# Token statistics by ACT's running sums, earlier first scores, and a new spread of work in an attention + MLP kernel

## The chip, the cores and the metric

The kernel runs on one core of a Trainium2 chip. The metric is the device time of one execution in microseconds (us). All times here are us unless marked ns. The engines carry the profile's names: PE is TensorE (matmuls), PEld its weight loads, DVE is VectorE, ACT is ScalarE, POOL is GpSimd, SP is SyncE, which here only issues DMAs.

## The reference

The input `x` has 2048 tokens of 512 channels. An attention of 32 heads with 16 channels each looks back over a window of 256 tokens; an MLP of width 1792 runs behind a layer norm; a gate of one number per token mixes the two. All is in fp32.

```python
def _A_ref(x, wqkv, wo):                     # attention
    H = 32; Dh = D // H; W = 256
    qkv = (x @ wqkv).reshape(B, S, 3, H, Dh).transpose(2, 0, 3, 1, 4)
    q, k, v = qkv[0], qkv[1], qkv[2]
    scores = jnp.einsum("bhqd,bhkd->bhqk", q, k) * (Dh ** -0.5)
    mask = (idx[:, None] - idx[None, :] >= 0) & (idx[:, None] - idx[None, :] < W)
    p = softmax(jnp.where(mask[None, None], scores, -1e9))
    o = jnp.einsum("bhqk,bhkd->bhqd", p, v)
    return o.transpose(0, 2, 1, 3).reshape(B, S, D) @ wo

def _B_ref(x, w1, b1, w2, b2):               # MLP
    m = jnp.mean(x, axis=-1, keepdims=True)
    v = jnp.var(x, axis=-1, keepdims=True)
    y = (x - m) / jnp.sqrt(v + 1e-5)
    h = gelu(y @ w1 + b1)                    # tanh form
    return h @ w2 + b2

g = sigmoid((x * gate_w).sum(-1, keepdims=True))
return g * _A_ref(x, wqkv, wo) + (1 - g) * _B_ref(x, w1, b1, w2, b2)
```

## The kernel before, in words

**Numbers.** Each fp32 operand of a matmul is split in a high part (`copy`, L122, on ACT) and the rest (`lo_part`, L119, on DVE or POOL); a product is then three matmuls: high x high, high x low, low x high.

**Three stages.** The *first stage* (0 to about 155 us) makes q, k and v. It is a list of 48 *units*, n = 0 to 47, each of which is one output tile of 12 matmuls (`qk_unit`, L289, or `v_unit`, L319) into one of four PSUM buffers `ps_d`. Between the units other work is put in by a table: `at(n, fn)` lets `fn` run ahead of unit n, and `after(k, fn)` lets it run k units later. The order in which the program calls an engine is the order in which that engine does its work, so these numbers set the order on every engine at once. The *loop* (about 155 to 505) does the attention and the MLP's first product by the letters of `ORDER`: S is a pair of score products for the row maxima, T a pair of transposed scores for the exponentials, P a product with v, f one step of the MLP. One letter is one *spot*. `soon(n, fn)` lets `fn` run n spots later. The *end stage* multiplies by `wo` and `w2`.

**q and k.** `qk_out` (L293) copies and splits a finished tile and stores the parts to DRAM (`put`, L300). `load_stacks` (L325) reads the *stacks* back to the SBUF tile `qk`, in two DMAs at L330; the first call takes the tokens 0 to 511 of the first four heads. `s_pair` (L334) makes the scores of one block of 128 queries with up to 384 keys (L343) in one of two PSUM buffers `ps_x`, and DVE masks (L352) and reduces them (L353) to the maxima `mx`. Ten blocks of the first four heads, two pairs each, are made in the first stage: ahead of the units 16, 19, 22 ... 43.

**The maxima.** After every fourth block `put_max` (L357) splits the maxima on POOL, turns them on DVE (`turn`, `ms`), writes them to DRAM (`put`, L371, `md`) and reads them back as two rows of the stacks (L377, two DMAs, `qk<-md`), from where the T matmuls (L398) take them. In the loop these four steps run at the spots of `CHAIN` after the fourth block: 6, 13, 17 and 34.

**Statistics, gate and y.** `stat_unit(i)` loads 128 tokens (`in_xa`, L440), and three units later DVE makes mean and variance (L444, L445) and the gate's dot product (L446). `stat_end` (L451) has DVE start and POOL finish, in four Newton steps, the inverse root of eight blocks' variances, and stores it. `load_y` (L481) reads mean and inverse root back for 1024 tokens, and then for eight slices (64 channels of each of two halves): load, subtraction of the mean on POOL (L503), multiplication on DVE (L496), copy on ACT, low part on DVE. A slice starts in each unit from 26, and from 34 for the other half of the tokens.

**Other names.** `t2()` (L82) gives the next of `nt` = 15 buffers `t`; whoever takes one waits until its last user is done. `load_w` (L206) loads the other q and k weights (`in_wqk`, L209). `load_w1` loads the MLP's weights, `double` (L308) copies q or k rows within DRAM, `hp` (L635) holds the MLP's first product. SP issues nearly all DMAs, one after the other.

The table's lines that the change touches, and the lines around them:

```python
    at(11, load_consts)
    for c in range(NCH):
        at((12, 22, 33, 44)[c], lambda c=c: load_stacks(0, c * C, C))
    for i in range(NB):
        at(11 + i, lambda i=i: stat_unit(i))
    at(21, lambda: stat_end(0))
    at(29, lambda: stat_end(1))
    at(25, lambda: load_y(0, 0, KT))
    at(33, lambda: load_y(1, 0, KT))
    for qb in range(NB - LAG):
        at(16 + 3 * qb, lambda qb=qb: [s_pair(0, qb, pr) for pr in range(2)])
```

Of the kernel before, what the change touches and what calls it, by code (L numbers as in the profile page):

```python
# [16 lines left out]
AF = mybir.ActivationFunctionType  # L17
ALU = mybir.AluOpType

S = 2048  # L20
D = 512
# [4 lines left out]
KT = D // 64  # L26
FT = F // 128
C = 512
# [6 lines left out]
EPS = 1e-5  # L35
# [13 lines left out]
         "ffTSfffTfSffSPTfSfTffSffTSfffTSfffSSfffTffffTffffTfTPPTTPTfTffTfTffffTfTffPfTTPTfTffTfTfffTffTfPfTTP"  # L49
         "TT")  # L50
LAG = 6
CHAIN = (6, 13, 17, 34)


@with_exitstack
def gated_mix_kernel(ctx, tc: tile.TileContext, xt, x2, wq0, wqk, wv, wo, xa, gw, w1, w2, b1, b2, out):
    nc = tc.nc
    dve, act, pool, pe, sp = nc.vector, nc.scalar, nc.gpsimd, nc.tensor, nc.sync
# [59 lines left out]
    def lo_part(lo, src, hi, eng=dve):  # L118
        eng.tensor_tensor(out=lo, in0=src, in1=f32(hi), op=ALU.subtract)  # L119

    def copy(dst, src):
        act.activation(dst, src, AF.Copy)  # L122
# [4 lines left out]
    def after(k, fn):  # L127
        todo.setdefault(step[0] + k, []).append(fn)
# [17 lines left out]
    stat = dram.tile([2, 2, S // 2], F32, name="stat")  # L146
# [14 lines left out]
    mv = consts.tile([128, NB, 2], F32, name="mv")  # L161
# [3 lines left out]
    get("edge", "edge", 1, (128, 104))  # L165
    open_pool("x", "right")
    open_pool("work")
    nt[0] = 15
    gws = get("work", "gws", 1, (128, D))

    def x8():
        return get("x", "x8", 10, (128, 2048), F32R)
# [152 lines left out]
    def load_stacks(p, a, n):  # L325
        g, j = divmod(p, 2)
        held_cols[p] = a + n
        for t in (1, 0):
            src = view(qkd[g, t], [S, 98], [100 * S, 2], [1, n], off=4 * j * 50 * S + a)
            sp.dma_start(f32(qk[14:112, 2 * t:2 * t + 2, a:a + n]), f32(src))  # L330

    mxs, done = {}, set()
# [105 lines left out]
    def stat_unit(i):  # L438
        s = t2()
        sp.dma_start(s, xa[i])  # L440

        def rest():
            st = small("st", 2, (128, 6))
            dve.bn_stats(st, s)  # L444
            dve.bn_aggr(mv[:, i, :], st)  # L445
            dve.scalar_tensor_tensor(out=s, in0=s, scalar=1.0, in1=gws, op0=ALU.mult, op1=ALU.mult,  # L446
                                     accum_out=z[:, i:i + 1])

        after(3, rest)

    def stat_end(half):  # L451
        ve = small("ve", 2, (128, NB // 2))
        u = small("u", 2, (128, NB // 2))
        m = mv[:, half * 8:half * 8 + 8]
        r = rt[:, half, 1]
        ri = r.bitcast(I32)
        dve.tensor_scalar(ve, m[:, :, 1], EPS, None, op0=ALU.add)
        dve.tensor_scalar(ri, ve.bitcast(I32), 1, None, op0=ALU.logical_shift_right)
        dve.tensor_scalar(ri, ri, -1.0, float(0x5f3759df), op0=ALU.mult, op1=ALU.add)
        for _ in range(4):  # L460
            pool.tensor_tensor(out=u, in0=r, in1=r, op=ALU.mult)
# [3 lines left out]
        pool.tensor_copy(rt[:, half, 0], m[:, :, 0])  # L465
# [12 lines left out]

    ys = {}

    def load_y(cp, s0, s1, gap=2):  # L481
        mr = [t2() for _ in range(2)]
        for j in range(2):
            for e in range(2):
                sp.dma_start(mr[j][64 * e:64 * e + 64], view(stat, [0, 64], [1, C], off=cp * S + j * 2 * C + e * C))

        def one(s):
            if (cp, 0, s // 4) not in ys:
                for k in range(2):
                    ys[cp, k, s // 4] = x8()  # L490
            h, l = (ys[cp, k, s // 4][:, s % 4 * C:s % 4 * C + C] for k in range(2))
            x = t2()
            sp.dma_start(x, x2[cp, :, s * C:(s + 1) * C])

            def rest():
                dve.tensor_tensor(out=x, in0=x, in1=mr[1], op=ALU.mult)  # L496
                copy(h, x)

            def fin():
                lo_part(l, x, h)  # L500
                done.add(("y", cp, s))

            after(2, lambda: pool.tensor_tensor(out=x, in0=x, in1=mr[0], op=ALU.subtract))  # L503
            after(3, rest)
            after(4, fin)

        for s in range(s0, s1):
            after(1 + (s - s0) * gap // 2, lambda s=s: one(s))

    w1t = {}  # L510

    def load_w1(f, eng=pool):
        w, raw = [wt(), wt()], t2()
        w1t[f] = w
        sp.dma_start(raw, w1[f])
# [28 lines left out]
    rest = [QK(g, t, c) for c in range(NCH) for g in range(1, NG) for t in range(2)]  # L544
# [4 lines left out]
    def at(n, fn):  # L549
        plan.setdefault(n, []).append(fn)  # L550
# [5 lines left out]
    for i in range(4):  # L556
        at((3, 5, 6, 8)[i], lambda i=i: pool.memset(vs[:, 4 * i:4 * i + 4], 1.0))
    at(2, masks)
    at(11, load_consts)
    for g in range(NG):  # L560
        at((8, 16, 20, 24)[g], lambda g=g: gaps(g))
    for c in range(NCH):
        at((12, 22, 33, 44)[c], lambda c=c: load_stacks(0, c * C, C))
    for i in range(NB):
        at(11 + i, lambda i=i: stat_unit(i))
    at(21, lambda: stat_end(0))
    at(29, lambda: stat_end(1))
# [278 lines left out]
    for n in range(len(seq)):  # L846
        tick()
        for k in (n + 6,):
            c, f = item(k)
# [4 lines left out]
        c, f = item(n + 1)  # L854
# [59 lines left out]
```

## Time and profile before

| | |
|---|---|
| median of 3 runs | 712.82 (710.83 to 714.23) |
| the profiled execution | 716.88, of which its span 715.2 |
| granted TensorE clock, mean | 0.992 |
| PE busy | 694.1 (97%), 5740 matmuls |
| DVE busy | 484.3 (68%) |
| ACT busy | 365.8 (51%) |
| POOL busy | 270.6 (38%) |
| DMA | 137.92 MB, mean 193 GB/s |

How the rows of the profile read: in the lists of groups and of waits a row has the engine, the source line, the operation and `out<-in` by the program's names (with buffer numbers left out), then how many there were, their busy time and the mean ns of one, and behind the last bar the idle time ahead of them and what ended it. In a timeline a row begins with the start and the length in us, and a bracket holds the idle time just before it and its releaser. SPq is SP's queue of DMA issues. In a row of windows, each engine has its busy time and its count of instructions; behind them stand the granted TensorE clock, the DMA engines' share, and GB/s.

### The profile page before, as it was taken

The page shows a single profiled execution, that of the slowest core. Times are in us where ns is not written, and L with a number is a line of the kernel's source. Part 1 is how long each engine was busy: PE and PEld are TensorE (multiplying, and loading weights), DVE is VectorE, ACT ScalarE, POOL GpSimd, SP SyncE. Part 2 cuts the span into 40 slices and gives each one's busy share as a digit, 9 for nine tenths or more (in the row PEclk, how much of TensorE's full clock was granted, in tenths as well). Part 3 has the DMA queues.
Part 4 walks back from the last instruction along what each step waited for, and adds up shares of the span by engine and source line. Part 5 has one row for each costly group of instructions (what it writes and reads, how often), then busy time and mean ns, then how long its engine had stood idle before and what let it go on. Part 6 is the DMA issues. An engine that isn't in the chain of part 4 may idle for free.

```text
span 715.2 us, 15880 instructions
## 1 busy us (share of the span) xinstructions
PE 694.1 (97%) x5740; PEld 542.3 (76%) x5740; DVE 484.3 (68%) x996; ACT 365.8 (51%) x581; POOL 270.6 (38%) x631
## 2 busy tenths in 40 slices
PE   9999989799999989999999999999999999999997
PEld 6877767577677767777777778777677788888886
DVE  7639877877786858868767677784375745735554
ACT  6422223247668667667775767768543413224121
POOL 9600173506467456556654656658200000000000
PEclk9999999999999999999999999999999999999999
DMA  8998959677556657656867564544775544442531
GB/s 316 337 287 247 297 179 270 194 220 221 192 179 194 189 196 217 190 189 175 238 186 204 158 202 149 173 120 151 239 241 152 175 140 144 153 138 99 191 112 59
DMA packets 102533, 137.92 MB, mean 193 GB/s; under 512 B 13912, under 2 KB 53528, under 8 KB 102328
## 3 DMA queue, kind: packets, MB, share of 16 engines
q1 hardware_dynamic: 97848, 128.79, 57.7%
q10 hardware_dynamic: 4608, 8.13, 3.8%
q8 instruction: 46, 0.75, 0.4%
q14 instruction: 31, 0.25, 0.1%
HBM read 81.53 MB, written 54.30 MB: 190 GB/s over the span
## 4 chain that ended last, share of the span: by engine, by line
PE 65%; DMA 15%; DVE 7%; SPq 5%; issue 3%; ACT 2%; POOL 2%; ACTq 0%; DVEq 0%; POOLq 0%
PE ps_b L622 20%; PE ps_a L833 16%; PE ps_b L417 11%; PE ps_b L398 7%; PE ps_b L343 6%; PE ps_o L812 6%; DMA t<-in_wqk 2%; DMA qk<-t 2%; DMA qk<-md 1%; DMA v<-in_xt 1%; DVE t L496 1%; DMA t<-stat 1%; DMA t<-hp 1%; DVE t L119 1%; SPq L300 1%
## 5 line engine op out<-in xcount | busy, mean ns | idle before, releaser
L622 PE MATMUL ps_b<-x,w 64*128 64x512 f32 x1344 | 215.6, 398 | 0.5 <-ACT p L400 0.2
L402 POOL TENSOR_SCALAR_AFFINE_SELECT p<-p 128x256 f32<-128x256 f32 x344 | 132.4, 414 | 111.2 <-ACT p L400 109.8
L400 ACT ACTIVATE p<-ps_b 128x768 f32<-128x768 f32 (+2 forms) x184 | 137.6, 770 | 45.8 <-PE ps_b L398 37.7
L833 PE MATMUL ps_a<-x,t 128*128 128x512 f32 x648 | 151.0, 390 | 0.3 <-DVE t L682 0.2
L353 DVE TENSOR_REDUCE mx<-ps_b 128x2 f32<-128x512 f32 x208 | 144.1, 693 | 7.2
L833 PEld LDWEIGHTS ps_a<-x,t 128*128 128x128 f32 x648 | 121.2, 188 | 27.3 <-DVE t L119 1.2
L622 PEld LDWEIGHTS ps_b<-x,w 64*128 64x128 f32 x1344 | 132.3, 188 | 12.0 <-issue 2.8
L352 DVE COPY_PREDICATED ps_b<-tri,ps_b 128x256 f32<-128x256 uint8 x208 | 88.3, 425 | 55.3 <-PE ps_b L343 39.5
L398 PE MATMUL ps_b<-qk 64*128 64x384 f32 (+5 forms) x512 | 92.1, 347 | 5.8 <-DMA qk<-md 4.9
L289 PE MATMUL ps_d<-x,w 128*128 128x512 f32 x360 | 88.5, 398 | 0.0
L343 PE MATMUL ps_b<-qk 62*128 62x384 f32 (+3 forms) x472 | 86.4, 347 | 0.6 <-ACT v L122 0.5
L289 PEld LDWEIGHTS ps_d<-x,w 128*128 128x128 f32 x360 | 67.9, 191 | 16.0 <-issue 1.7
L417 PE MATMUL ps_b<-p,v 128*32 128x256 f32 (+1 forms) x1376 | 74.4, 329 | 0.9 <-ACT p L400 0.9
L398 PEld LDWEIGHTS ps_b<-qk 64*128 64x128 f32 (+1 forms) x512 | 52.1, 186 | 26.3 <-issue 9.5
L122 ACT ACTIVATE t<-ps_b 128x512 f32<-128x512 f32 (+1 forms) x112 | 52.0, 491 | 39.1 <-PE ps_b L417 33.8
L402 POOL TENSOR_SCALAR_AFFINE_SELECT x<-x 128x256 f32<-128x256 f32 x136 | 52.1, 410 | 38.1 <-ACT x L400 37.5
L400 ACT ACTIVATE x<-ps_b 128x768 f32<-128x768 f32 (+2 forms) x72 | 55.3, 778 | 19.4 <-PE ps_b L398 15.2
L417 PEld LDWEIGHTS ps_b<-p,v 128*32 128x32 f32 x1376 | 38.7, 109 | 26.7 <-ACT p L400 4.1
L343 PEld LDWEIGHTS ps_b<-qk 62*128 62x128 f32 (+1 forms) x472 | 47.6, 187 | 14.9 <-issue 3.6
L119 DVE TENSOR_TENSOR t<-t,t 128x512 fp32r<-128x512 f32 x70 | 48.5, 692 | 14.6 <-ACT t L122 11.6
L122 ACT ACTIVATE t<-t 128x512 fp32r<-128x512 f32 x16 | 10.1, 632 | 79.1 <-DVE t L800 54.8
L678 ACT ACTIVATE t<-t,b1s 128x512 f32<-128x512 f32 x56 | 38.0, 715 | 24.0 <-DMA t<-hp 23.5
(81 smaller groups left out, 662.3 us busy)
## 6 DMA issues: line engine op xcount, KB each, us to landing
qk<-qk SPq DMA_DIRECT2D x112, 196.0 KB
t<-hp SPq DMA_DIRECT2D x56, 256.0 KB
hp<-t SPq DMA_DIRECT2D x52, 256.0 KB
qk<-t SPq DMA_DIRECT2D x48, 256.0 KB
osc<-t SPq DMA_DIRECT2D x31, 256.0 KB
t<-in_w SPq DMA_DIRECT2D x28, 256.0 KB
w<-w SPq DMA_DIRECT2D x28, 256.0 KB
qk<-t ACTq DMA_DIRECT2D x24, 256.0 KB
```

What stands on the lines that cost most here:

```text
L119: eng.tensor_tensor(out=lo, in0=src, in1=f32(hi), op=ALU.subtract)
L122: act.activation(dst, src, AF.Copy)
L289: pe.matmul(o, a[:, dt * 128:(dt + 1) * 128], b[:, dt * C:(dt + 1) * C], start=n == 0, stop=n == 11)
L343: pe.matmul(o[:, e, :n], qs[pr][r:k, qb * 128:qb * 128 + 128], ks[pr][r:k, t0:t0 + n], start=True, stop=True)
L352: dve.copy_predicated(o[:, :, :128], tri, o[:, :, 256:384])
L353: dve.tensor_reduce(m, o[:, :, :256], mybir.AxisListType.X, ALU.max)
L398: pe.matmul(o[:, e, :w], ks[pr][r:k, kb * 128:kb * 128 + 128], qs[pr][r:k, kb * 128:kb * 128 + w], start=True, stop=True)
L400: act.activation(pt[:, :, :w], o[:, :, :w], AF.Exp, scale=0.25)
L402: pool.affine_select(out=pt[:, :, a:a + 128], in_=pt[:, :, a:a + 128], pattern=[[0, 2], [sgn, 128]], base=b, channel_multiplier=-sgn, comp ...
L417: pe.matmul(a[32 * h:32 * h + 32, at:at + w], vs[:, kb, v:v + 32], pts[p, kb][:, h, fr:fr + w], start=n == 0, stop=n == len(parts) - 1, sk ...
L622: pe.matmul(o[:, e], w[kt // 4][r:r + 64, k, m:m + 128], y[r:r + 64, a:a + C], start=n == 0, stop=n == 23)
L833: pe.matmul(accs[c][b], x[:, b * 128:(b + 1) * 128], w, start=f == 0 and n == 0, stop=f == FT - 1 and n == 2)
```

## The change

The mean and variance of a token are made on ACT by two activations with running sums: a copy scaled by -1/512, whose sum is the negative mean, and a square with that as bias, whose sum is 512 times the variance. Their full outputs go to a new tile `waste`, for which the ring of `t` buffers has 14 instead of 15. The dot product stays on DVE, one unit later. `stat_end` scales the variance on DVE, and POOL does three Newton steps in place of four; the subtraction of the mean becomes an addition. The blocks of tokens are loaded one unit earlier, from unit 10. The two tables of statistics for y are read at units 25 and 32, and the y slices start at the units 24, 25, 26, 28, 29, 30, 31, 32 and 33 to 40, with lags of 3 and 2 units up to the subtraction. The stacks are loaded ahead of the units 11, 19, 28, 44 instead of 12, 22, 33, 44, and the ten blocks of scores are made ahead of the units 14, 16, 18, 21, 23, 25, 28, 30, 33, 36. The MLP's first two weights are loaded one unit earlier. In the loop the maxima are read back 28 instead of 34 spots after their block.

```diff
-CHAIN = (6, 13, 17, 34)
+CHAIN = (6, 13, 17, 28)
...
-    nt[0] = 15
+    nt[0] = 14
     gws = get("work", "gws", 1, (128, D))
+    waste = get("work", "waste", 1, (128, D))
...
         sp.dma_start(s, xa[i])
 
-        def rest():
-            st = small("st", 2, (128, 6))
-            dve.bn_stats(st, s)
-            dve.bn_aggr(mv[:, i, :], st)
+        def sums():
+            act.activation(waste, s, AF.Copy, scale=-1.0 / D, accum_out=mv[:, i, 0:1])
+            act.activation(waste, s, AF.Square, bias=mv[:, i, 0:1], accum_out=mv[:, i, 1:2])
+
+        def dot():
             dve.scalar_tensor_tensor(out=s, in0=s, scalar=1.0, in1=gws, op0=ALU.mult, op1=ALU.mult,
                                      accum_out=z[:, i:i + 1])
 
-        after(3, rest)
+        after(3, sums)
+        after(4, dot)
...
-        dve.tensor_scalar(ve, m[:, :, 1], EPS, None, op0=ALU.add)
+        dve.tensor_scalar(ve, m[:, :, 1], 1.0 / D, EPS, op0=ALU.mult, op1=ALU.add)
...
-        for _ in range(4):
+        for _ in range(3):
...
-    def load_y(cp, s0, s1, gap=2):
-        mr = [t2() for _ in range(2)]
+    mr = {}
+
+    def load_mr(cp):
+        mr[cp] = [t2() for _ in range(2)]
         for j in range(2):
             for e in range(2):
-                sp.dma_start(mr[j][64 * e:64 * e + 64], view(stat, [0, 64], [1, C], off=cp * S + j * 2 * C + e * C))
+                sp.dma_start(mr[cp][j][64 * e:64 * e + 64], view(stat, [0, 64], [1, C], off=cp * S + j * 2 * C + e * C))
...
-            after(2, lambda: pool.tensor_tensor(out=x, in0=x, in1=mr[0], op=ALU.subtract))
-            after(3, rest)
-            after(4, fin)
-
-        for s in range(s0, s1):
-            after(1 + (s - s0) * gap // 2, lambda s=s: one(s))
+        after(lag, lambda: pool.tensor_tensor(out=x, in0=x, in1=mr[cp][0], op=ALU.add))
+        after(lag + 1, scale)
+        after(lag + 2, low)
...
-    at(11, load_consts)
+    at(10, load_consts)
...
-        at((12, 22, 33, 44)[c], lambda c=c: load_stacks(0, c * C, C))
+        at((11, 19, 28, 44)[c], lambda c=c: load_stacks(0, c * C, C))
     for i in range(NB):
-        at(11 + i, lambda i=i: stat_unit(i))
+        at(10 + i, lambda i=i: stat_unit(i))
     at(21, lambda: stat_end(0))
     at(29, lambda: stat_end(1))
+    at(25, lambda: load_mr(0))
+    at(32, lambda: load_mr(1))
+    for i in range(KT):
+        at((24, 25, 26, 28, 29, 30, 31, 32)[i], lambda i=i: load_y(0, i, 3))
+        at(33 + i, lambda i=i: load_y(1, i, 2))
...
-    at(25, lambda: load_y(0, 0, KT))
-    at(33, lambda: load_y(1, 0, KT))
-    at(39, lambda: load_w1(0, dve))
-    at(42, lambda: load_w1(1, dve))
+    at(38, lambda: load_w1(0, dve))
+    at(41, lambda: load_w1(1, dve))
     for qb in range(NB - LAG):
-        at(16 + 3 * qb, lambda qb=qb: [s_pair(0, qb, pr) for pr in range(2)])
+        at((14, 16, 18, 21, 23, 25, 28, 30, 33, 36)[qb], lambda qb=qb: [s_pair(0, qb, pr) for pr in range(2)])
```

Three places show how rows move. Line numbers of the changed kernel are one to five higher than those of before for the same operation. The first place is SP's queue behind its first 28 rows, which are the same in both: `in_wqk` are weights of q and k, `in_xa` blocks of tokens, `qk_1_66` and `qk_0_67` stored q and k parts, `qk_79` the SBUF tile of the stacks. Before:

```order
L435 DMA gws_99<-in_gw 128x512
L436 DMA b1s<-in_b 128x14
L440 DMA t_463<-in_xa 128x512
L209 DMA t_466<-in_wqk 128x512
L330 DMA qk_79<-qk_1_66 98x2x512
L330 DMA qk_79<-qk_0_65 98x2x512
L440 DMA t_486<-in_xa 128x512
```

The same place after:

```order
L436 DMA gws_99<-in_gw 128x512
L437 DMA b1s<-in_b 128x14
L441 DMA t_448<-in_xa 128x512
L331 DMA qk_79<-qk_1_66 98x2x512
L331 DMA qk_79<-qk_0_65 98x2x512
L441 DMA t_468<-in_xa 128x512
L210 DMA t_471<-in_wqk 128x512
```

The stacks stand one row higher: one `in_wqk` that was ahead of them is now behind them, with a block of tokens between.

The second place is DVE from the last short instruction of the second half's `stat_end` (on `rt`). `x_161` and the like are high and low parts of y, `t_869` and `t_891` the inverse roots read back, `ps_d` the units' outputs, `ps_x` score pairs. Before:

```order
L459 TENSOR_SCALAR rt<-rt 128x8
L119 TENSOR_TENSOR x_162_912<-t_913,x_161_911 128x512
L496 TENSOR_TENSOR t_938<-t_938,t_869 128x512
L119 TENSOR_TENSOR t_1067<-ps_d_1053,t_1066 128x512
L119 TENSOR_TENSOR x_162_912<-t_938,x_161_911 128x512
L496 TENSOR_TENSOR t_962<-t_962,t_869 128x512
L467 STREAM_TRANSPOSE ms_1028<-rt 128x32
L352 COPY_PREDICATED ps_x_1080<-tri,ps_x_1080 128x2x128
L353 TENSOR_REDUCE mx_588<-ps_x_1080 128x2
```

After:

```order
L462 TENSOR_SCALAR rt<-rt 128x8
L119 TENSOR_TENSOR x_144_863<-t_896,x_143_862 128x512
L501 TENSOR_TENSOR t_930<-t_930,t_891 128x512
L353 COPY_PREDICATED ps_x_1057<-tri,ps_x_1057 128x2x128
L354 TENSOR_REDUCE mx_543<-ps_x_1057 128x2
L353 COPY_PREDICATED ps_x_1062<-tri,ps_x_1062 128x2x128
L354 TENSOR_REDUCE mx_543<-ps_x_1062 128x2
L119 TENSOR_TENSOR t_1086<-ps_d_1072,t_1085 128x512
L119 TENSOR_TENSOR x_144_863<-t_930,x_143_862 128x512
L470 STREAM_TRANSPOSE ms_1031<-rt 128x32
L369 STREAM_TRANSPOSE ms_1068<-nm_1067 128x32
```

Before, two multiplications of y (L496) stand between the end of the statistics and the next score pair; after, one (L501) does, and the next multiplication comes behind the transposes.

The third place is SP around the tenth write of maxima in the loop. `md` are the maxima in DRAM, `osc` and `hp` stored results, `w<-w` a swap of the MLP's weights within SBUF, the row at L310 or L311 a `double`. Before:

```order
L371 DMA md_2934<-ms_2933 4x32x32
L430 DMA osc<-t_2883 128x512
L519 DMA w_2854<-w_2853 64x1024 x2
L635 DMA hp<-t_3052 128x512
L635 DMA hp<-t_3054 128x512
L330 DMA qk_79<-qk_1_68 98x2x256
L330 DMA qk_79<-qk_0_67 98x2x256
L310 DMA qk_1_70<-qk_1_70 16x8x512
L377 DMA qk_79<-md_2934 2x2x512 x2
```

After:

```order
L372 DMA md_2911<-ms_2910 4x32x32
L431 DMA osc<-t_2862 128x512
L378 DMA qk_79<-md_2911 2x2x512 x2
L521 DMA w_2833<-w_2832 64x1024 x2
L640 DMA hp<-t_3031 128x512
L640 DMA hp<-t_3033 128x512
L331 DMA qk_79<-qk_1_68 98x2x256
L331 DMA qk_79<-qk_0_67 98x2x256
L311 DMA qk_1_70<-qk_1_70 16x8x512
```

The reading back of the maxima stands seven DMAs higher, one other row behind the write.

More of the change, by code (lines that the diff above doesn't have):

```diff
@@ L479, in gated_mix_kernel, with load_y, scale, low @@
     ys = {}
-    def load_y(cp, s0, s1, gap=2):
-        mr = [t2() for _ in range(2)]
+    mr = {}
+    def load_mr(cp):
+        mr[cp] = [t2() for _ in range(2)]
         for j in range(2):
             for e in range(2):
-                sp.dma_start(mr[j][64 * e:64 * e + 64], view(stat, [0, 64], [1, C], off=cp * S + j * 2 * C + e * C))
[L487 to L503, printed above, removed]
-            after(3, rest)
-            after(4, fin)
-        for s in range(s0, s1):
-            after(1 + (s - s0) * gap // 2, lambda s=s: one(s))
+                sp.dma_start(mr[cp][j][64 * e:64 * e + 64], view(stat, [0, 64], [1, C], off=cp * S + j * 2 * C + e * C))
+    def load_y(cp, s, lag):
+        if (cp, 0, s // 4) not in ys:
+            for k in range(2):
+                ys[cp, k, s // 4] = x8()
+        h, l = (ys[cp, k, s // 4][:, s % 4 * C:s % 4 * C + C] for k in range(2))
+        x = t2()
+        sp.dma_start(x, x2[cp, :, s * C:(s + 1) * C])
+        def scale():
+            dve.tensor_tensor(out=x, in0=x, in1=mr[cp][1], op=ALU.mult)
+            copy(h, x)
+        def low():
+            lo_part(l, x, h)
+            done.add(("y", cp, s))
+        after(lag, lambda: pool.tensor_tensor(out=x, in0=x, in1=mr[cp][0], op=ALU.add))
+        after(lag + 1, scale)
+        after(lag + 2, low)
     w1t = {}
```

## Prediction

> All times are us, and a "unit" is the stretch of 12 matmuls between two positions of the first stage. I read the page's first part, then TensorE's waits, then windows with the granted clock, then the timeline at each wait.
>
> **What bounds the kernel now.**
>
> ```profile
> PE 694.1 (97%) x5740; PEld 542.3 (76%) x5740; DVE 484.3 (68%) x996; ACT 365.8 (51%) x581; POOL 270.6 (38%) x631
> ```
>
> TensorE is idle for 715.2 - 694.1 = 21.1. The change removes no matmul, so it can win only PE's waits and slow matmuls behind them, and it can lose by making waits. Who ends them (total, times, longest):
>
> ```profile
> PE ps_x L343 <- DVE mx L353: 6.3, 7, 2.1
> PE ps_b L398 <- DMA qk<-md: 4.9, 3, 2.5
> PE ps_b L398 <- DVE ms L368: 0.6, 1, 0.6
> PE ps_x L343 <- DMA qk<-qk: 0.5, 1, 0.5
> ```
>
> The first group is the first stage's score pairs, which have two PSUM buffers and wait until DVE has reduced the pair before. The next two are the returns of the maxima (the 0.6 I count with them: a return of maxima was in flight there). The last is the first load of the stacks. Windows (length, then busy time of PE, PEld, DVE, ACT, POOL, granted clock, DMA share, GB/s):
>
> ```profile
> 45.00:51.00 6.00, 5.49 (x25) 4.21 (x24) 2.75 (x6) 1.72 (x3) 0.00 (x0) 1.00 1.04 248
> 51.00:94.00 43.00, 42.98 (x195) 34.00 (x196) 36.46 (x102) 9.47 (x16) 6.36 (x21) 1.00 0.92 285
> 94.00:143.00 49.00, 42.58 (x180) 32.41 (x179) 37.75 (x58) 14.27 (x28) 26.52 (x34) 0.97 0.69 204
> 139.50:144.00 4.50, 4.50 (x15) 3.52 (x14) 3.67 (x5) 1.24 (x3) 1.78 (x1) 0.62 0.56 166
> 389.00:393.00 4.00, 4.00 (x24) 3.72 (x24) 2.43 (x6) 2.15 (x5) 1.88 (x6) 0.57 0.64 205
> ```
>
> Until 94 PE is full; 94 to 143 holds the DVE waits; and three times the clock falls to half for some 3.4 (the first and the last are the two last rows: a mean of 0.62 over 4.5). PE's own rows show what such a dip costs and what stands ahead of it:
>
> ```profile
> 44.88 2.88 PE L319 MATMUL ps_d<-wv,x 128*128 128x512 f32 x12
> 47.60 2.88 PE L289 MATMUL ps_d<-x,w 128*128 128x512 f32 x12
> 51.02 0.44 PE L343 MATMUL ps_x<-qk 62*128 62x128 f32 x4 [0.54 <-DMA qk<-qk]
> ...
> 138.08 0.44 PE L343 MATMUL ps_x<-qk 62*128 62x384 f32 x2 [2.15 <-DVE mx L353]
> ...
> 139.52 4.61 PE L289 MATMUL ps_d<-x,w 128*128 128x512 f32 x12
> ...
> 253.02 0.69 PE L398 MATMUL ps_b<-qk 64*128 64x384 f32 x2 [2.55 <-DMA qk<-md]
> ...
> 387.18 0.45 PE L398 MATMUL ps_b<-qk 64*128 64x384 f32 x2 [1.44 <-DMA qk<-md]
> ```
>
> A unit is 47.60 - 44.88 = 2.72. Twelve matmuls took 4.61 at half clock against 2.88: 1.7 lost, each of three times behind a wait of 1.44 or more (the three rows with brackets from 138 on).
>
> Why DVE is late, from its rows and POOL's:
>
> ```profile
> 102.75 1.75 DVE L496 TENSOR_TENSOR t<-t,t 128x512 f32<-128x512 f32 x1 [3.46 <-POOL t L503]
> 104.55 0.39 DVE L352 COPY_PREDICATED ps_x<-tri,ps_x 128x256 f32<-128x256 uint8 x1
> ```
>
> ```profile
> 95.69 0.57 POOL L461 TENSOR_TENSOR u<-rt 128x8 f32<-128x8 f32 x1 [1.13 <-DVE rt L459]
> ...
> 101.28 0.19 POOL L465 COPY rt<-mv 128x8 f32<-128x8 f32 x1
> 101.43 5.42 POOL L503 TENSOR_TENSOR t<-t,t 128x512 f32<-128x512 f32 x4
> ```
>
> DVE stood 3.46 before a y slice, whose subtraction stood on POOL behind the Newton steps (95.69 to 101.47), and the score pair behind that slice is reduced only from 104.55. With 37.75 busy of the 49 from 94 to 143, and idle times of its own between, DVE doesn't get that back: the longest of PE's waits for it stands at 138.
>
> **The change, part by part.** Durations (busy, mean ns):
>
> ```profile
> L444 DVE BATCH_NORM_STATS2 st<-t 128x6 f32<-128x512 f32 x16 | 10.9, 683 | 6.0 <-DMA t<-in_xa 6.0
> L445 DVE BATCH_NORM_AGGREGATE mv<-st 128x2 f32<-128x6 f32 x16 | 2.9, 182 | 0.6
> L446 DVE SCALAR_TENSOR_TENSOR t<-t,gws 128x512 f32<-128x512 f32 x16 | 10.8, 678 | 0.0
> L446 DVE DVE_READ_ACCUMULATOR t<-t,gws 128x1 f32 x16 | 1.3, 82 | 0.0
> L496 DVE TENSOR_TENSOR t<-t,t 128x512 f32<-128x512 f32 x16 | 17.5, 1094 | 3.5 <-POOL t L503 3.5
> L119 DVE TENSOR_TENSOR x<-t,x 128x512 fp32r<-128x512 f32 x16 | 11.8, 739 | 3.4 <-ACT x L122 3.4
> L119 DVE TENSOR_TENSOR t<-ps_d,t 128x512 fp32r<-128x512 f32 x22 | 15.1, 685 | 6.0 <-ACT t L122 6.0
> L353 DVE TENSOR_REDUCE mx<-ps_x 128x2 f32<-128x512 f32 x16 | 11.1, 693 | 0.5
> L122 ACT ACTIVATE x<-t 128x512 fp32r<-128x512 f32 x16 | 10.1, 632 | 42.1 <-DVE t L496 42.1
> L678 ACT ACTIVATE t<-t,b1s 128x512 f32<-128x512 f32 x56 | 38.0, 715 | 24.0 <-DMA t<-hp 23.5
> ```
>
> *Sums on ACT.* DVE loses 16 x (0.68 + 0.18) = 13.8. ACT gains 32 instructions: a copy like the 0.63 row, and a square with a bias per partition like the 0.715 row. No row of ACT has a running sum; its price lies between nothing and DVE's read of an accumulator, 0.08. The nearest row is the latter, so 16 x (0.63 + 0.72 + 0.16) = 24. They fall into units 13 to 28, where ACT was busy for 9.5 of 43, and a `qk` copy behind them may be late by three units, since there are four `ps_d` buffers: nothing on the path. If an `xa` load lands late, ACT stands where DVE stood (6.0 above); the same three units cover it.
>
> Here the Trainium skill speaks against the change: ScalarE: Activation LUTs, Rules for kernel authors, sends adding and multiplying to VectorE. By it the move trades 13.8 of DVE for 24 of ACT, some 10 lost. The windows above decide otherwise: from 94 on DVE ends PE's waits and ACT has room.
>
> *Fewer Newton steps* take 4 of 16 operations from POOL, about (101.28 - 95.69) / 4 = 1.4 each half. *The y slices* now leave a gap behind the second half's Newton steps: the slice after them is multiplied two units later, so the 3.46 goes.
>
> *DVE's account from unit 28*, starting 1.3 behind PE (copy 0.6, low part 0.69), with dot 0.76, multiply 1.09, low part of y 0.74, two reductions 2.2 (0.69 and the 0.39 of 104.55, twice), and 0.9 for the short ones (an estimate: six, none above L445's 0.18): the pair of unit 28 is reduced at 5.3, of 30 at 13.2, of 33 at 20.8. PE (2.72 a unit, 0.6 a pair) asks for them at 6.0, 14.8 and 23.6. So no wait. If each multiply took 1.75, as beside POOL above, it would be 6.0, 15.2, 24.1: up to 0.8 in all. I keep 0.5: **-6.3 + 0.5 = -5.8**, and the dip behind the 2.15 goes: **-1.7**. After unit 36 DVE is some two units behind, four `ps_d` buffers cover it.
>
> *First pairs at unit 14, stacks at unit 11.* SyncE before:
>
> ```profile
> 40.03 0.43 SPq L440 DMA_DIRECT2D t<-in_xa  x1
> 40.51 0.45 SPq L209 DMA_DIRECT2D t<-in_wqk  x1
> 41.06 0.83 SPq L330 DMA_DIRECT2D qk<-qk  x2
> ```
>
> Its first 28 rows are the same in both programs and stand one behind the other, so moving the stacks one unit up moves them past one DMA only, the `in_wqk` of 256 KB. At the 285 GB/s of 51 to 94 that is 0.9, at the 248 of 45 to 51 1.06; I take 0.9. They landed at 51.02, so now at 50.1. PE however asks for them at the start of unit 14, 44.88: a wait of 5.2 in place of 0.5, **+4.7**. The bounds: 0 were the queue empty, 5.6 were nothing won. A dip follows, as it did behind shorter waits: **+1.7**. Behind it nothing is hurt: DVE, ACT and the DMAs gain on PE.
>
> On dips the Trainium skill (TensorE: Matmul & The Clock Gate, The HAM clock gate) asks for an idle window of about 3.4, free-running. Here waits of 1.44 to 2.55 were enough, so the measurement decides; it bears on rival (5).
>
> *The other stack loads* (units 19, 28) keep four and five units to their pairs; the maxima of the first two blocks are sent earlier, and SP stands there when idle. *One `t` buffer less*: the tightest new user is the `y` load of unit 35, which waits for the subtraction of that unit and is used two units later: nothing, at worst one unit of SP. *w1 a unit earlier*: nothing.
>
> *Maxima read back at 28.* 30 of 32 returns move six spots up on SP, some 1.7 (350 for the 1202 letters):
>
> ```profile
> 239.81 0.58 SPq L371 DMA_DIRECT2D md<-ms  x1
> 242.11 0.36 SPq L430 DMA_DIRECT2D osc<-t  x1
> ...
> 249.40 1.37 SPq L377 DMA_DIRECT2D qk<-md  x2
> ...
> 379.42 0.60 SPq L371 DMA_DIRECT2D md<-ms  x1
> ...
> 384.35 1.35 SPq L377 DMA_DIRECT2D qk<-md  x2
> ```
>
> At 249.40 the return came behind seven transfers that now stand behind it; it can go at about 243, and the 2.55 ends, as do the 0.6 and the remaining 4.9 - 2.55 - 1.44 = 0.9, which have the same order. The 1.44 stays: there SP waited until 384.35 for the write itself, which no order helps. **-4.1**, and the dip behind the 2.55: **-1.7**.
>
> **Sum.** The profiled execution took 716.88: -5.8 - 1.7 + 4.7 + 1.7 - 4.1 - 1.7 = -6.9, 710.0. The median of the runs is 712.82, 4.1 below it. The first four terms (-1.1) hang on queue order and should recur; the last two (-5.8) hang on when a DMA landed, and the lower median says that a usual run has less of them. I take half: 712.82 - 1.1 - 2.9 = **708.8**.
>
> **Rivals.** (1) SyncE becomes the bound: a return directly behind its write stands until that lands, up to 4.9 above, and the stack loads behind it are late. It decides the time once a load has less than that left between its issue and its use. Against it: of all first uses of stacks only the very first waits now (the 0.5 of the waits' list), though the list doesn't say by how much the others make it. Three loads late by 2, each with a dip: 711.7 + 3 x 3.7 = 722.8, where 711.7 = 712.82 - 1.1. (2) The first stacks are hidden anyway: 708.8 - 6.4 = 702.4; the full DMA share at 45 to 51 (1.04) speaks against it. (3) The change leaves DVE behind all the same, since its account is within 1 of PE at unit 30: without the 7.5 of the first two terms, 716.3. (4) The returns win nothing, as other transfers hold them: 711.7. (5) No dip follows the wait at unit 14, as none followed most of the waits listed above (three dips in all): 708.8 - 1.7 = 707.1. By the clock gate's rule that depends on where a free-running window falls, and a wait of 5.2 holds a whole one of 3.4 in about half of the cases.
>
> **Chances.** Likeliest 0.40, (1) 0.13, (2) 0.08, (3) 0.14, (4) 0.16, (5) 0.09. The range leaves out (1) alone: 702 to 717. The likeliest case alone is 706 to 711. About 0.5%, 3.6, is what a measurement tells from no change: faster means below 709.26. That holds (2), (5) and six tenths of the likeliest: 0.41; slower, above 716.4, (1) and half of (3): 0.20; the rest 0.39.
>
> **What would show it.** Right: one PE wait of about 5 at some 45, ended by `qk<-qk`, with half clock behind; no L343 wait on DVE over 0.5; `md` waits below 2 in all. Wrong: L343 waits on DVE of several us remain; stack waits appear after 160; or PE runs through unit 14, which would break the largest loss in the sum.

## The result, and the profile after

The changed kernel takes 719.21 us (median of 8 runs, 716.28 to 721.91), the kernel before 713.07 in the same runs (8, 710.83 to 715.74). The ratio is 1.0082, with a 95% interval of 1.0055 to 1.0109: 5.9 us slower. The forecast was 708.8, with a range of 702 to 717, so the time lies outside of the range and on the other side of no change.

The profiled execution took 721.91 (span 720.2). Its first part, and TensorE's waits (total, times, longest):

```profile
PE 698.6 (97%) x5740; PEld 541.7 (75%) x5740; DVE 472.7 (66%) x964; ACT 388.5 (54%) x645; POOL 268.6 (37%) x623
```

```profile
PE ps_x L344 <- DMA qk<-qk: 4.2, 1, 4.2
PE ps_b L344 <- ACT p L401: 3.1, 1, 3.1
...
PE ps_b L399 <- DMA qk<-md: 1.4, 2, 1.2
PE ps_d L290 <- ACT v L122: 1.3, 2, 0.9
PE ps_d L320 <- DVE t L119: 1.1, 1, 1.1
...
PE ps_x L344 <- DVE mx L354: 0.6, 1, 0.6
...
PE ps_d L290 <- DVE t L119: 0.3, 1, 0.3
```

Most of what the prediction named as signs of being right is there: one wait at unit 14 for the stacks (4.2), 1.4 in place of 4.9 for the return of the maxima, and 0.6 in place of 6.3 for DVE's maxima in the first stage, a little above the 0.5 that it had set. What it did not name are the rows that are new: 2.7 for `ps_d`, the units' output buffers, and 3.1 for ACT's exponentials. PE's rows show where they stand:

```profile
49.81 0.59 PE L344 MATMUL ps_x<-qk 62*128 62x128 f32 x4 [4.16 <-DMA qk<-qk]
...
137.45 5.78 PE L290 MATMUL ps_d<-x,w 128*128 128x512 f32 x24 [0.36 <-ACT v L122]
...
144.34 3.06 PE L320 MATMUL ps_d<-wv,x 128*128 128x512 f32 x12 [1.12 <-DVE t L119]
148.31 3.03 PE L290 MATMUL ps_d<-x,w 128*128 128x512 f32 x12 [0.91 <-ACT v L122]
151.62 3.04 PE L290 MATMUL ps_d<-x,w 128*128 128x512 f32 x12 [0.29 <-DVE t L119]
...
166.53 0.69 PE L344 MATMUL ps_b<-qk 62*128 62x384 f32 x2 [3.12 <-ACT p L401]
```

Two waits have a stretch of half clock behind them (windows; the third last number is the granted clock):

```profile
49.50:54.00 4.50, 4.19 (x14) 3.38 (x15) 1.30 (x8) 2.06 (x5) 0.00 (x0) 0.62 1.04 386
...
166.00:171.00 5.00, 4.47 (x24) 3.88 (x26) 2.36 (x5) 2.21 (x4) 2.62 (x8) 0.50 0.51 177
```

The first of these stretches lasted 3.4, as each of the three before the change did. The second lasted 6.8 (from 166 to 174 the granted clock was 0.57), so it costs about 3.4 and not 1.7.

Since PE does the same 5740 matmuls in both, one can ask at which time each is begun. That tells where the 5.0 between the two spans came from:

| PE begins | before | after | after is behind by |
|---|---|---|---|
| unit 13 | 42.16 | 42.69 | 0.5 |
| unit 17 | 54.23 | 60.74 | 6.5 |
| unit 29 | 89.89 | 97.72 | 7.8 |
| unit 44 | 143.97 | 144.34 | 0.4 |
| unit 47, the last | 152.16 | 154.70 | 2.5 |
| matmul 700, early in the loop | 163.81 | 171.71 | 7.9 |
| matmul 3392 in the loop | 392.63 | 395.53 | 2.9 |
| end of the span | 715.2 | 720.2 | 5.0 |

Three of the steps were forecast. The first is 6.0 lost at unit 14 (6.4 in the sum): 3.6 more of wait (4.16 in place of 0.54), 1.7 of half clock, and some 0.6 for the matmuls of one more block of scores. The second is 7.4 won back by unit 44, of which 1.3 are the matmuls of two blocks of scores that the changed kernel makes ahead of unit 29 already, so 6.1 of waits and dips (7.5). The third is 5.0 won in the loop, where the returns of the maxima are (5.8, of which the forecast took half). Three steps were not forecast: 2.1 behind unit 44, 5.4 at the start of the loop, and a drift that has no wait to its name, with 0.5 ahead of unit 13, some 0.6 of the 1.3 between the units 17 and 29 (the rest is the other block of scores), and 2.1 behind matmul 3392.

### The profile page after: what moved, and what is told of

Same layout as the page of the kernel before. It is cut to its first block, busy times and chain, and to the rows that moved or that the text cites. A ratio compares the mean times of both kernels' runs of the same rounds, so it can differ in the third digit from the quotient of the medians.

```text
span 720.2 us, 15939 instructions
## 1 busy us (share of the span) xinstructions
PE 698.6 (97%) x5740; PEld 541.7 (75%) x5740; DVE 472.7 (66%) x964; ACT 388.5 (54%) x645; POOL 268.6 (37%) x623
## 3 DMA queue, kind: packets, MB, share of 16 engines
q10 hardware_dynamic: 4608, 8.13, 3.7%
## 4 chain that ended last, share of the span: by engine, by line
PE 67%; DMA 12%; DVE 8%; SPq 5%; ACT 4%; issue 3%; POOL 1%; ACTq 1%; DVEq 0%; POOLq 0%
PE ps_b L627 19%; PE ps_a L838 16%; PE ps_b L418 11%; PE ps_b L399 6%; PE ps_b L344 6%; PE ps_o L817 6%; DMA qk<-qk 3%; DVE t L501 2%; DVE x L119 2%; ACT t L122 1%; PE ps_d L290 1%; SPq L301 1%; DMA md<-ms 1%; ACT x L122 1%; DMA qk<-t 1%
## 5 line engine op out<-in xcount | busy, mean ns | idle before, releaser
L627 PEld LDWEIGHTS ps_b<-x,w 64*128 64x128 f32 x1344 | 132.5, 188 | 12.3 <-issue 2.8
L290 PE MATMUL ps_d<-x,w 128*128 128x512 f32 x360 | 86.9, 396 | 1.6 <-ACT v L122 1.3
L344 PEld LDWEIGHTS ps_b<-qk 62*128 62x128 f32 x472 | 47.6, 187 | 19.8 <-ACT p L401 5.9
L119 DVE TENSOR_TENSOR t<-t,t 128x512 fp32r<-128x512 f32 x70 | 48.5, 693 | 14.9 <-ACT t L122 11.6
```

What stands on the lines that cost most here:

```text
L290: pe.matmul(o, a[:, dt * 128:(dt + 1) * 128], b[:, dt * C:(dt + 1) * C], start=n == 0, stop=n == 11)
L344: pe.matmul(o[:, e, :n], qs[pr][r:k, qb * 128:qb * 128 + 128], ks[pr][r:k, t0:t0 + n], start=True, stop=True)
L627: pe.matmul(o[:, e], w[kt // 4][r:r + 64, k, m:m + 128], y[r:r + 64, a:a + C], start=n == 0, stop=n == 23)
```

## The experiments

Each ratio is to the kernel before, from runs on the same chip; its interval is of 95%. The median of the kernel before lay between 713.1 and 715.9 from one set of runs to the next, so kernels are compared by their ratios.

**The first scores.** Theory Y was that the chain of y on DVE and ACT bounds the second half of the first stage, so that time lost at unit 14 is lost for good; rival Q that SyncE's queue does, and hides it.

```diff
-        at((14, 16, 18, 21, 23, 25, 28, 30, 33, 36)[qb], ...
+        at((16, 17, 18, 21, 23, 25, 28, 30, 33, 36)[qb], ...
```

> The changed kernel, with the first two blocks of scores ahead of units 16 and 17 instead of 14 and 16; all else as in the changed kernel. Theory Y: the second half of the first stage is bound by y's chain (multiply on DVE, copy on ACT, the unit's own copy behind it on ACT, low parts on DVE: 3.6 us a slice in the changed kernel against 2.72 a unit), so what is lost at unit 14 moves the chain's first slice and with it the end of the stage one to one. It expects the 4.2 wait and the dip behind it to go, the first multiplication at about 91.5 instead of 97.6, the stage's end some 6 earlier, and 713 us. Rival Q: the end of the stage is set by SyncE, whose loads of y stand behind stores of q and k that wait for DVE; then PE's lost time at unit 14 is hidden by the later waits, the stage ends within 1.5 of now, and the time is 717.5 to 719.5.

Measured: 713.21, ratio 1.0000 (0.9975 to 1.0024), 0.8% under the changed kernel. The time lost at the first scores is not hidden, and Q as it was put is refuted. But the way there isn't quite the one expected, as PE's rows of this run show:

```profile
50.99 0.44 PE L344 MATMUL ps_x<-qk 62*128 62x128 f32 x4
51.36 3.03 PE L290 MATMUL ps_d<-x,w 128*128 128x512 f32 x12
56.09 0.83 PE L344 MATMUL ps_x<-qk 62*128 62x256 f32 x4 [1.70 <-DVE mx L350]
56.84 4.61 PE L320 MATMUL ps_d<-wv,x 128*128 128x512 f32 x12
```

The stacks are in time for unit 16, but three blocks of scores in three units make PE wait 1.70 for DVE, with a unit at half clock (4.61) behind it. PE began unit 17 at 56.84 against 60.74, and unit 47 at 150.45 against 154.70, so 3.9 gained became 4.3; the waits for `ps_d` remained (0.8, 0.7 and 0.3). The wait for the exponentials was gone, which this edit does not explain by itself; that is taken up at the last run.

**Score and stack tables alone**, on the kernel before:

```diff
-        at((12, 22, 33, 44)[c], lambda c=c: load_stacks(0, c * C, C))
+        at((11, 19, 28, 44)[c], lambda c=c: load_stacks(0, c * C, C))
...
-        at(16 + 3 * qb, lambda qb=qb: [s_pair(0, qb, pr) for pr in range(2)])
+        at((14, 16, 18, 21, 23, 25, 28, 30, 33, 36)[qb], lambda qb=qb: ...
```

> The kernel before, with the changed tables of score blocks and stack loads alone. Theory Y: PE waits 4 to 5 us at unit 14 with a dip behind it, y's chain starts 6 later, and the whole comes out at 718 to 720, as the changed kernel does: the other parts of the change are then worth about nothing together. Rival: the waits of the score pairs for DVE (6.3) are slack that takes the loss up, since DVE gets more time: 712 to 715.

Measured: 720.68, ratio 1.0088 (1.0060 to 1.0117). PE's waits:

```profile
PE ps_b L398 <- DMA qk<-md: 7.3, 5, 2.2
PE ps_x L343 <- DMA qk<-qk: 4.6, 1, 4.6
...
PE ps_x L343 <- DVE mx L353: 2.0, 2, 1.4
...
PE ps_d L319 <- DVE t L119: 1.1, 1, 1.1
```

The two tables alone cost what the whole change costs. And they alone turn 4.3 of the 6.3 of waiting for the maxima away, while waits for `ps_d` come up: earlier scores let PE run ahead of DVE until the four output buffers are full, and there it stands instead. (The waits for the returned maxima, 7.3 in this execution against 4.9, are longer as well.)

**The maxima's return**, undone in the changed kernel and done alone in the kernel before:

```diff
-CHAIN = (6, 13, 17, 28)
+CHAIN = (6, 13, 17, 34)
```

> The changed kernel with the maxima read back at spot 34 as before. If the earlier reading back was worth the 4 us that the prediction gave it at most, 722 to 724 and md waits of 3 to 5 us; if it was worth half, 721; if it is worth nothing or costs (its wait for its own write holds up SyncE), 717 to 719.5.

Measured: 724.67, ratio 1.0116 (1.0059 to 1.0172), with 4.9 of waits for the returned maxima (`qk<-md`) in three places. The interval overlaps that of the changed kernel (1.0055 to 1.0109), so this run alone doesn't tell the two apart.

> The kernel before with the maxima read back at spot 28; nothing else. The run with spot 34 in the changed kernel makes the earlier reading back worth about 5 there. If that carries over: md waits under 2 in the loop, 708 to 710. If it is worth something only behind the other changes, 713 to 715. If SyncE standing at its own write costs stack loads, over 716.

Measured: 711.05, ratio 0.9940 (0.9912 to 0.9969): a gain of 4.3, between 2.2 and 6.3. The md waits of this run are in one row:

```profile
PE ps_b L398 <- DMA qk<-md: 0.4, 1, 0.4
```

The earlier return has a price, too. All nine kernels here that read the maxima back at spot 28 make PE wait for stacks in the loop (`ps_b` <- `qk<-qk`), 0.5 to 3.0 in all and 1.8 in this one; the lists of the six with spot 34 show no such wait.

**ACT's running sums alone**, on the kernel before (with the tile `waste`, 14 `t` buffers, and the dot product, the loads and the constants moved as in the change):

```diff
-        after(3, rest)
+        after(3, sums)
+        after(4, dot)
```

> The kernel before with mean and variance by ACT's running sums alone (and what hangs on it: the tile of waste, 14 t buffers, the dot product a unit later, the token loads and constants a unit earlier, the sign of the mean); four Newton steps, old tables. The prediction's account of DVE would take some 8 of its 13.8 us off ahead of unit 28 and the waits of the score pairs with them: 706 to 709. Theory Y (what counts is the ping-pong of DVE and ACT per slice of y from unit 29 on, and POOL's Newton steps, none of which this touches): the waits for the maxima stay above 4 us, 712 to 716.

Measured: 717.24, ratio 1.0033 (1.0008 to 1.0058), above both ranges. The waits for the maxima did fall, from 6.3 to 2.4, as the prediction's account had it and theory Y had not; PE began unit 47 2.3 earlier than before. But the time is not shorter: the returns took 6.2 in this execution, and matmuls were slower, as the runs on the place in SBUF show below.

**The copy of y.** In the changed kernel's rows DVE and ACT take turns. DVE:

```profile
140.63 1.79 DVE L501 TENSOR_TENSOR t<-t,t 128x512 f32<-128x512 f32 x1
143.60 0.69 DVE L119 TENSOR_TENSOR t<-ps_d,t 128x512 fp32r<-128x512 f32 x1 [1.18 <-ACT t L122]
144.20 0.68 DVE L119 TENSOR_TENSOR x<-t,x 128x512 fp32r<-128x512 f32 x1
144.80 1.78 DVE L501 TENSOR_TENSOR t<-t,t 128x512 f32<-128x512 f32 x1
```

ACT:

```profile
142.45 0.63 ACT L122 ACTIVATE x<-t 128x512 fp32r<-128x512 f32 x1 [3.06 <-DVE t L501]
142.99 0.58 ACT L122 ACTIVATE t<-ps_d 128x512 fp32r<-128x512 f32 x1
```

ACT copies a y slice only when DVE has multiplied it, the unit's own output waits behind that copy on ACT, and DVE waits for the unit's output: 144.80 - 140.63 = 4.2 in this round, against the 2.75 of a unit (two take 5.50 in the run with the later copy, below). The multiplication took 1.79 here, beside an addition on POOL:

```profile
140.34 1.52 POOL L508 TENSOR_TENSOR t<-t,t 128x512 f32<-128x512 f32 x1 [0.45 <-DMA t<-in_x]
```

Where it took 0.69, a round took 3.1; the six rounds between the multiplications at 131.39 and 152.1 took 3.45 in the mean. In the stretch from 80 to 165 that wait of DVE comes to

```profile
DVE t L119 <- ACT t L122: 12.4, 11, 2.2
```

in the changed kernel, and before to

```profile
DVE t L119 <- ACT t L122: 5.2, 5, 1.2
```

The next edit issues the copy of y one unit later, behind the unit's output; it was made in the kernel before and in the changed one.

```diff
             dve.tensor_tensor(out=x, in0=x, in1=mr[cp][1], op=ALU.mult)
-            copy(h, x)
 
         def low():
+            copy(h, x)
             lo_part(l, x, h)
```

> The kernel before, with ACT's copy of a y slice issued one unit later, directly ahead of its low part and so no longer between the multiplication and the unit's own copy; nothing else is moved. Theory Y: DVE's waits of 1.2 for ACT ahead of the units' low parts go, a slice takes about 3 instead of 3.9, most of the 6.3 us in which PE waits for the maxima goes and the dip at 140 with it: 705 to 709. Rival Q: DVE's lateness comes from loads and stores on SyncE, and the order of the copies changes nothing: 712 to 714.

Measured: 712.32, ratio 0.9975 (0.9954 to 0.9996): a gain, but 1.8 and not 6. DVE's wait for the units' outputs fell to 0.8, but its wait for the copies of y rose from 3.4 to 6.3; the 3.7 before POOL's subtraction and 4.3 of PE's waits for the maxima stayed. In the kernel before, the edit moved most of DVE's waiting for ACT and removed little of it.

> The changed kernel, with ACT's copy of a y slice issued one unit later, directly ahead of its low part; the first scores stay at unit 14. Theory Y: DVE's 12.4 us of waiting for ACT's copies of units falls under 4, so PE's waits at units 42 to 47 (2.7) go, and the last stores of q and k leave early enough that the exponentials at 163 do not wait (3.1 and the half clock behind it, 1.7): 711 to 714, with the 4.2 at unit 14 still there. Rival Q (DMA traffic and SyncE at the end of the stage, with other causes than DVE's lateness): the wait at 163 stays, 717 to 719.5.

Measured: 710.28, ratio 0.9946 (0.9926 to 0.9966), 1.4% under the changed kernel. PE goes through the last units without a wait:

```profile
141.54 2.96 PE L320 MATMUL ps_d<-wv,x 128*128 128x512 f32 x12
144.34 5.67 PE L290 MATMUL ps_d<-x,w 128*128 128x512 f32 x24
149.84 2.96 PE L320 MATMUL ps_d<-wv,x 128*128 128x512 f32 x12
```

Unit 47 begins at 149.84 and not at 154.70, and the wait for the exponentials is gone too. DVE's own wait fell less than expected, to 7.5. So the `ps_d` waits come from the order of these two copies; whether the second wait does, this run cannot say, since the edit also shifted which `t` buffers lie where.

**The buffer of the second exponentials.** ACT's third exponential, the first into its second buffer, waited in the changed kernel for a store, one of the two last of the stage that SyncE sent (ACT's row, then SyncE's):

```profile
165.67 1.51 ACT L401 ACTIVATE p<-ps_b 128x768 f32<-128x768 f32 x2 [3.97 <-DMA qk<-t]
```

```profile
158.23 3.63 SPq L301 DMA_DIRECT2D qk<-t  x2
```

In the compiled program that buffer stands where the `t` with the low part of unit 45 stood, and waits until its store has read it. In the kernel with the first scores at 16 and 17, and in that with the later copy, it stands on buffers whose stores are earlier. The last run leaves the copy where the change had it, and gives the second and third tiles the two spare buffers:

```diff
-        return extra[n // 4] if n in (3, 6) else first.pop() if first else new_p()
+        return extra[n - 2] if n in (2, 3) else first.pop() if first else new_p()
```

> The changed kernel, with the order of the seven buffers for exponentials changed: the second and third tile are the two spare ones in x8, and the tile that stands on the last stores' t buffers comes fourth instead of second. All else as in the changed kernel, the copy of y too. If the 3.1 at 163 and the half clock behind it come from that buffer alone (ACT waits until a low part's store, issued by SyncE at 158, has left it): that wait goes, PE's waits in units 42 to 47 (2.7) stay, and the time is 5 less than the changed kernel's, 713.5 to 715 (ratio to before 1.000 to 1.003). If lateness of DVE itself is the cause, PE waits at another place by as much, and the ratio stays at 1.006 to 1.009.

Measured: 716.68, ratio 1.0037 (1.0005 to 1.0069). The exponentials go through (`x` is the spare buffer), and the waits for `ps_d` are what they were in the changed kernel:

```profile
159.86 0.81 ACT L401 ACTIVATE x<-ps_b 128x768 f32<-128x768 f32 x1 [0.47 <-PE ps_b L399]
160.91 0.81 ACT L401 ACTIVATE x<-ps_b 128x768 f32<-128x768 f32 x1 [0.24 <-PE ps_b L399]
```

```profile
PE ps_d L290 <- ACT v L122: 1.3, 2, 0.9
...
PE ps_d L320 <- DVE t L119: 1.1, 1, 1.1
```

Between unit 47 and matmul 700 this execution took 163.68 - 152.41 = 11.3, the changed kernel 171.71 - 154.70 = 17.0 and the one before 11.7. So the wait hangs on the buffer: DVE waits for ACT as long here as in the changed kernel (12.3 and 12.4), and the wait for the exponentials is gone. The two other kernels with the buffer in that place waited there too, 3.4 in the one with the maxima at spot 34 and 3.1 in the one with 64 bytes more that follows, and no other kernel did. Whether it would also go with DVE in time and the buffer left where it is, no run tells. The half clock doesn't come with it each time: behind the 3.4 the granted clock stayed at 1.00. By the ratios 3.2 came off, give or take 3 (an estimate from the two intervals), where the traces have 5.7 at that place; 3.0 of waits for stacks in the loop, which the profile of the changed kernel has at 0.5, came up in this execution.

**The place in SBUF.** The drift without waits stands in the matmuls themselves. Two units, 24 matmuls, before and after:

```profile
34.01 5.60 PE L319 MATMUL ps_d<-wv,x 128*128 128x512 f32 x24
```

```profile
34.29 5.76 PE L320 MATMUL ps_d<-wv,x 128*128 128x512 f32 x24
```

The change no longer needs the two small tiles `st`, 64 bytes per partition in the first pool, so the large tiles behind it lie 64 bytes lower (in the compiled program the weights `w` from 4608 instead of 4672, the stacks from 29184 instead of 29248); the ten tiles with the parts of `x` and y stay where they were. Two runs tell this apart from all else: the changed kernel with 64 unused bytes, and the kernel before with `st` put into another tile's buffers.

```diff
+    consts.tile([128, 16], F32, name="pad")
```

> The changed kernel with 64 bytes per partition more in the pool of constants, never used: the change freed 64 there (the two tiles st), which moved every large tile of SBUF down by 64. All traces of kernels without st have 2.77 to 2.80 us a unit ahead of unit 13 and 147.7 for the 640 matmuls 5050 to 5690 of the end; all with st have 2.72 and 145.9. If the place in SBUF is the cause: 2.72 and 145.9 again, and 716 to 717.5 in place of 719.2. Rival (ACT's sums, the tile of waste or the ring of 14 are the cause): 2.77 and 147.7 remain, 718.5 to 720.

```diff
-            st = small("st", 2, (128, 6))
+            st = small("scr", 2, (128, 256), BF16).bitcast(F32)[:, :6]
```

> The kernel before, with the statistics' tile st put into the buffers of the scratch tile scr (used on DVE alone at that time), so that all large tiles of SBUF stand 64 bytes lower, as in the changed kernel; the order of all work is that of before. If the place in SBUF is the cause: 2.77 us a unit up to unit 13, 147.7 for the matmuls 5050 to 5690, and 716 to 718. Rival: all as before, 713.5 to 715.

Measured: 719.27, ratio 1.0048 (1.0023 to 1.0072), for the first; 717.29, ratio 1.0029 (1.0004 to 1.0054), for the second. The first time alone would lie in its rival's range, but the kernel before took 715.91 in the same runs, and the rival's sign, the slower matmuls, is not there. Their rows, the changed kernel with the pad and then the kernel before without its 64 bytes:

```profile
34.25 5.60 PE L321 MATMUL ps_d<-wv,x 128*128 128x512 f32 x24
```

```profile
34.73 5.76 PE L319 MATMUL ps_d<-wv,x 128*128 128x512 f32 x24
```

The pace goes with the 64 bytes in both directions. In the end stage, too: between matmuls 5050 and 5690 PE took 145.9 before, 147.8 after, 146.1 with the pad, 147.7 before without the bytes; all fifteen traces of this case fall into two groups, 145.9 to 146.6 and 147.7 to 147.9. By the ratios the 64 bytes cost 2.1 (0.3 to 3.9) in the pair of the kernel before, and 2.4 in that of the changed one, where the two intervals leave some 2.6 either way (an estimate), so that this pair alone would not show it. The profiled execution with the pad isn't shorter than that of the changed kernel (720.6 and 720.2): its half clock at unit 14 lasted 6.8 and not 3.4. Why the matmuls care is not shown.

**Better versions.** The changed kernel with the copy later and the scores ahead of units 16, 18, 20, 22, 24, 26, 28, 30, 33 and 36:

> The changed kernel, with the copy of y a unit later as above, and the score blocks ahead of units 16, 18, 20, 22, 24, 26, 28, 30, 33, 36, so that neither the stacks (unit 14) nor DVE (three blocks in units 16 to 18) stop PE. Theory Y: no wait over 0.7 in the first stage, its end 6 to 8 earlier than before's, md waits under 2: 704 to 708. If the ping-pong is not what counts, it is as the kernel with the first blocks at 16 and 17 but without its 1.7 wait and dip: 710 to 712.

Measured: 710.26, ratio 0.9924 (0.9889 to 0.9959), a gain of 5.4, short of the 704 to 708 expected; the profiled execution, of span 702.4, had no wait over 0.2 from its first unit to 157. The same with the 64 bytes:

> The kernel with score blocks from unit 16 on and the later copy of y, with the same unused 64 bytes. If the place in SBUF is the cause: some 2.4 less than without them, 706.5 to 708.5, and a span of about 700; else 709.5 to 711.

Measured: 707.04, ratio 0.9878 (0.9846 to 0.9910). And the kernel before with two edits alone, the return at spot 28 and the later copy:

> The kernel before with two edits: maxima read back at spot 28, and ACT's copy of a y slice one unit later. If the two gains measured apart (3.6 and 2) add up: 708 to 710. If they overlap: 711 to 712.

Measured: 707.46, ratio 0.9886 (0.9856 to 0.9915), 8 less than before, where they brought 4.3 and 1.8 alone: the two gains add up at the least. ACT's sums, the Newton steps, the new spread of y and the new tables bring nothing beside these two that can be measured (0.9878 against 0.9886, both without the loss by the 64 bytes).

## Why the prediction was wrong, point by point

- **First scores at unit 14: right.** The forecast was 5.2 of wait in place of 0.5 and a dip, 6.4; measured were 4.16 in place of 0.54 and a dip, 5.3. The stacks landed at 49.8 (50.1 forecast), but PE asked for them at 45.65 and not at 44.88. Rival (2), hidden anyway, is out; the tables alone cost as much as the whole change. Rival (5) can happen: in the run with the other buffers the wait was 2.58 and the granted clock stayed 1.00. Which of the two happens is not a matter of the length alone, since 1.70 brought half clock in the first run. The Trainium skill (TensorE: Matmul & The Clock Gate, Part 1: The HAM clock gate) has a free-running window, which fits waits of like length with and without a dip; that an idle stretch of about 3.4 is needed for it, the 1.70 here contradicts.
- **The waits for the maxima: right up to unit 44, and then wrong.** 0.6 stayed where 0.5 was kept, and by unit 44 PE had won back 6.1 of the 7.5. The step that failed is the sentence behind it: "After unit 36 DVE is some two units behind, four `ps_d` buffers cover it." They don't: DVE's account took the busy times of its instructions one after the other (1.09 + 0.74 + 0.69 = 2.5 for a slice and a unit's output) and left out that it waits for ACT in each round. With 3.1 to 4.2 a round and 2.75 a unit, DVE falls further behind until the buffers are full at unit 42. That cost 2.7 of waits, gone in the kernel with the later copy.
- **"Behind it nothing is hurt": wrong at the start of the loop.** The 3.1 for the exponentials and the half clock, 5.4 together, are the largest miss. The wait comes from a buffer that the account didn't follow: of `t` it asked what the smaller ring does within the stage ("nothing, at worst one unit of SP"), not what is laid over it in the next.
- **The returns: right in kind; whether to halve them stays open.** The sum had 5.8, the forecast took 2.9; 5.0 in the trace, 4.3 (2.2 to 6.3) alone on the kernel before. The interval holds both. Rival (4), that they win nothing, is out. Rival (1), that loads of stacks come late behind them, happens at a small size: 0.5 to 3.0 of waits in a trace, where it had taken 11.1 with the dips.
- **ACT's sums: about as counted.** DVE's busy time fell by 11.6 (13.8 taken), ACT's rose by 22.7 (24 taken), although the read of a sum took 0.19 on ACT, above the bound of 0.08. Alone they made the waits for the maxima shorter, but not the time.
- **A term was missing:** 64 bytes of SBUF, 2.1 (0.3 to 3.9).

The three misses, 2.1, 5.4 and the drift of 3.2, are 10.7, and the sum without them has the sign of the forecast. The table accounts for 5.0; the medians differ by 6.1, and the 1.1 between is in no profile. Rival (3), DVE behind all the same, came nearest with 716.3, mostly by luck: of the 7.5 that it takes back 6.1 were won, and DVE's lateness cost 2.1 at another place.

Of the three signs that the prediction had named as right two came true and the third was missed by 0.1, while the time went the other way: they were signs of the foreseen terms alone. Of the signs of being wrong one showed, and small: 0.5 of waits for stacks after 160.

## What to carry to other kernels

A wait that is removed by letting one engine run ahead can come back at the next buffer that it fills: follow the account to the end of the stage, with the waits between two engines that take turns in each round, and not with busy times alone. Ask of each buffer that is freed late what is laid over it in the next stage. And look at the pace of the matmuls in both traces before any wait is blamed: two units in a row tell whether it is the same.

## What the runs showed of the hardware

A shift of the weights, the stacks and other large SBUF tiles by 64 bytes changed the pace of fp32 matmuls of 128x512 by 2 to 3% in the first stage (2.72 against 2.77 to 2.80 a unit of 12) and by 1.2% in the end stage (145.9 against 147.7).

Wherever the half clock came in the fifteen traces, the last few us of the span left out, it lasted 3.4 or 6.8. The length of a wait of PE doesn't tell which of the two follows, or whether one does: behind 1.44, 1.70 and 2.15 it lasted 3.4, behind 2.51, 3.12 and 3.13 it lasted 6.8, and behind 2.58 and 3.40 there was none.

Reading a running sum takes an instruction of its own, and on ACT it is twice as long as on DVE (ACT's two forms of the changed kernel, then DVE's):

```profile
L445 ACT ACTIVATE waste<-t,mv 128x512 f32<-128x512 f32 x16 | 11.6, 724 | 0.5
...
L444 ACT ACTIVATION_READ_ACCUMULATOR waste<-t 128x1 f32 x16 | 3.0, 188 | 0.0
L445 ACT ACTIVATION_READ_ACCUMULATOR waste<-t,mv 128x1 f32 x16 | 3.0, 187 | 0.0
...
L448 DVE DVE_READ_ACCUMULATOR t<-t,gws 128x1 f32 x16 | 1.3, 84 | 0.0
```
